# Attention and a squared-ReLU feed-forward: the first head pair in two token halves, GpSimd's loads behind it, and two units' value products moved back

## Chip, cores and metric

The kernel runs on one core of a Trainium2 chip. The metric is device time in microseconds (us) of one execution; lower is better. A profile records a single execution and gives its own span, which is a little shorter than the timed runs.

## What is computed

```python
# q, k, v: (8, 12, 448, 64) = batch, heads, tokens, head dimension; float32
scores = (1 / sqrt(64)) * q @ k.T
m = max(scores, axis=-1)
e = exp(scores - m)
attn = e / (sum(e) + exp(-m) + 1e-09)      # softmax with one more, empty, place
x = (attn @ v) as (3584, 768)              # tokens by heads * head dimension
h = x @ w_in                               # w_in: (768, 2048)
g = relu(h) ** 2
out = g @ w_out                            # w_out: (2048, 768), out float32
```

The kernel leaves out the maximum: with it both parts of the fraction scale alike, so it takes exp of the scores and adds 1 to their sum.

## The kernel before

The work is one instruction order, written out by hand: each engine (PE for matrix products, DVE and ACT for element work, POOL, SP) runs its own instructions in the order of the program, and waits on semaphores for the data of others. The attention is cut into units. A unit is one pair of heads and a range of query tokens; its scores come in two calls, `scores(u, et, 0)` and `scores(u, et, 1)`, for two chunks of 112 keys each. After them ACT takes the exp, DVE adds the chunks for the row sums, and `values` multiplies with v. The 448 tokens of a head lie as 112 partitions by 4 (`RUN = 4`, `P = 112`), four consecutive tokens in a partition.

Batch 0 is done in units 0 to 11: six pairs with the first 192 queries, then the same pairs with the other 256. Units 12 to 17 are batch 1, and from unit 18 on two units go together. In units 0 to 5 there is no product with `w_in` yet to fill PE, and `keep_warm(n)` issues n matmuls on zeros, whose results nobody reads. `drain`, from unit 7 on, issues parts of the products with `w_in` between the steps of a unit.

Loads. Pairs 0 to 2 of batch 0 come raw in float32, q from SP and k from ACT, one load for each pair and tensor (L92). They are cast on chip (`cast`, L142), transposed on PE against an identity (`transposes`, L151), and copied by DVE from PSUM to `qk`. All other q, k, v and weights of the first batches are loaded by GpSimd (POOL), which casts to float16 in the transfer (L81, L97, L103, L107). Their order in the program is: v of pairs 0 to 2 (`vn`), the identity, q and k of pair 3, of pairs 4 and 5, v of pairs 3 to 5, four eighths of `win`, q and k of batch 1's pairs 0 to 2, four more eighths, q and k of batch 1's pairs 3 to 5, v of batch 1. The tenth of these is POOL's issue L103 at 10.31 us, q and k of batch 1's pairs 3 to 5 are the seventeenth and eighteenth.

In the loop of units 0 to 11 (L451) a step is: scores of the first two chunks, the transposes of a later pair (`transpose_at`: unit i transposes pair i+1 of batch 0 up to unit 4; units 9 to 14 transpose pairs 0 to 5 of batch 1), scores of the other two chunks, then `values` of the unit before. Two units, an odd and an even before it, share one PSUM tile `xp`, which `normalise` empties before the next pair may write it. In the next loop (L495) unit 12 calls `scores(u, et, 0)`, then `transposes(1, 3)`, then half of the products left, then `scores(u, et, 1)`.

Of the kernel before, what the change touches and what calls it, by code (L numbers as in the profile page):

```python
# [8 lines left out]
FP32 = mybir.dt.float32  # L9
FP16 = mybir.dt.float16  # L10
AF = mybir.ActivationFunctionType
# [4 lines left out]
def kernel(  # L16
# [9 lines left out]
    nc = tc.nc  # L26

    B, H, S, D = q.shape
    NT, DM = out.shape
    DF = moe_w_in.shape[1]  # L30
    NPAIR = H // 2
    DCH = DM // 128
    NFFB = DF // 128
    RUN = 4
    P = S // RUN
# [8 lines left out]
    consts = ctx.enter_context(tc.tile_pool(name="consts", bufs=1))  # L44
# [4 lines left out]
    flat = ctx.enter_context(tc.tile_pool(name="flat", bufs=2))  # L49
# [22 lines left out]
    win_r = moe_w_in.rearrange("(c p) f -> p c f", p=128)  # L72
    wout_r = moe_w_out.rearrange("(c p) f -> p c f", p=128)

    whole, vns, qks, xts, naturals, stages = {}, {}, {}, {}, {}, {}

    def load_v(b, p0, p1):
        hs = slice(2 * p0, 2 * p1)
        if b not in vns:
            vns[b] = v_pool.tile([P, H, RUN, D], FP16, name="vn")  # L80
        nc.gpsimd.dma_start(out=vns[b][:, hs], in_=v_r[b, :, hs])  # L81

    def load_natural(b, p0, p1):

        raw = b == 0 and p1 <= 3
        for n, r in (("q", q_r), ("k", k_r)):
            src = r[b, :, 2 * p0:2 * p1]
            if raw:
                if p0 == 0:
                    whole[n] = e_pool.tile([P, RUN * S], FP32, name="et")  # L90
                t = whole[n][:, p0 * 512:(p0 + 1) * 512].rearrange("p (h t d) -> p h t d", h=2, t=RUN)
                (nc.sync if n == "q" else nc.scalar).dma_start(out=t, in_=src)  # L92
            else:
                if p0 % 3 == 0:
                    whole[n] = nat.tile([P, NPAIR, RUN, D], FP16, name=f"{n}n{p0 // 3}")
                t = whole[n][:, 2 * (p0 % 3):2 * (p0 % 3 + p1 - p0)]
                nc.gpsimd.dma_start(out=t, in_=src)  # L97
            for pr in range(p0, p1):
                naturals[n, b, pr] = t[:, 2 * (pr - p0):2 * (pr - p0) + 2]
# [39 lines left out]
            )  # L139


    def cast(b, pr):  # L142
        for name in "qk":
            f = flat.tile([P, 2, RUN, D], FP16, name=f"flat{name}")
            if b == 0 and pr == 0 and name == "k":
                nc.scalar.activation(out=f, in_=naturals[name, b, pr], func=AF.Copy)
            else:
                nc.vector.tensor_copy(f, naturals[name, b, pr])
            naturals[name, b, pr] = f

    def transposes(b, pr):  # L151
        tp = mp_tile(FP16)
        for i, name in enumerate("qk"):
            for s in range(RUN):
                for h in range(2):
                    nc.tensor.transpose(tp[64 * h:64 * h + 64, i, P * s:P * s + P],
                                        naturals[name, b, pr][:, h, s, :], ident[0:P, 0:P])
        if b not in qks:
            qks[b] = qk_pool.tile([128, 3, COLS], FP16, name="qk")
        parts = (0, S // 2, S) if b == 0 and pr == 0 else (0, S)  # L160
        for x, y in zip(parts, parts[1:]):
            nc.vector.tensor_copy(qks[b][:, 0:2, pr * S + x:pr * S + y], tp[:, :, x:y])

    def exp(out_, in_):
        nc.scalar.activation(out=out_, in_=in_, func=AF.Exp, scale=scale)  # L167
# [8 lines left out]
    def scores(u, et, c):  # L176
        b, pr, q0, n = u
        qk = qks[b]
        two = [] if n == S else s_psum.tile([P, 2, 512], FP32, name="sp")
        for kk in (2 * c, 2 * c + 1):  # L180
            sp = s_psum.tile([P, 2, 512], FP32, name="sp") if n == S else two
            if b in ON_PE:
                o = 0 if n == S else kk % 2 * n
                for h in range(2):
                    r = slice(64 * h, 64 * h + 64)
                    x = pr * S
                    nc.tensor.matmul(sp[:, h, o:o + n], qk[r, 1, x + P * kk:x + P * kk + P],  # L187
                                     qk[r, 0, x + q0:x + q0 + n], start=True, stop=True)
            else:
                for h in range(2):  # L190
                    for odd in range(2):
                        r = slice(64 * odd, 64 * odd + 64)
                        x = (2 * pr + h) * (S // 2)
                        kx = x + kk // 2
                        which = 1
                        if kk % 2 != odd:
                            which = 2
                            kx += kk % 2
                        nc.tensor.matmul(sp[:, odd, h * (S // 2):(h + 1) * (S // 2)],  # L199
                                         qk[r, which, kx:kx + 2 * P - 1:2], qk[r, 0, x:x + S // 2],  # L200
                                         start=True, stop=True)
            if n == S:
                exp(chunk(et, u, c, kk).rearrange("p (o x) -> p o x", o=2), sp[:, :, 0:S])
        if n < S:
            exp(et[:, 0:RUN * 2 * n].rearrange("p (c h x) -> p c h x", c=2, h=2)[:, c], two[:, :, 0:2 * n])
# [24 lines left out]
    def values(u, et, xp, o=0):  # L230
        b, pr, _, n = u
        for kk in range(RUN):
            for h in range(2):
                nc.tensor.matmul(xp[64 * h:64 * h + 64, o:o + n], vns[b][:, 2 * pr + h, kk, :],  # L234
                                 of_head(chunk(et, u, kk // 2, kk), u, h), start=(kk == 0), stop=(kk == RUN - 1))
# [119 lines left out]
    for pr in range(3):  # L355
        load_natural(0, pr, pr + 1)
    nc.scalar.preload_act_table_set("natural_log_exp_and_others")
    load_v(0, 0, 3)
    ident = consts.tile([128, 128], FP16)
    make_identity(nc, ident)  # L360
    load_natural(0, 3, 4)
    load_natural(0, 4, 6)
    load_v(0, 3, 6)
# [28 lines left out]
    def left():  # L392
        return sum(t[0] for t in ins)
# [19 lines left out]
    units = [(0, pr, 0, FIRST) for pr in range(NPAIR)] + [(0, pr, FIRST, S - FIRST) for pr in range(NPAIR)]  # L413
# [8 lines left out]
    def keep_warm(n):  # L422
        wp = m_psum.tile([128, 512], FP32, name="mp")
        for _ in range(n):
            nc.tensor.matmul(wp, warm[:, 0:128], warm, start=True, stop=True)

    share = [0.0]
    ets, ess, rcps = {}, {}, {}
    xp = None
# [12 lines left out]
        return units[i], ets[i], es, half  # L442

    keep_warm(9)
    cast(0, 0)
    transposes(0, 0)
    keep_warm(3)
    cast(0, 1)


    for i in range(2 * NPAIR):  # L451
        u, et, es, half = begin(i)
        two = units[i - 2:i] if i and i % 2 == 0 else None
        if i % 2:
            xp = x_psum.tile([128, 512], FP32, name="xp")
        mode[0] = COLS2
        scores(u, et, 0)
        if i == 0:
            keep_warm(4)
        if i == NPAIR:  # L460
            values(units[i - 1], ets.pop(i - 1), xp, units[i - 1][3])
            rcp = row_sums(two, (ess.pop(i - 2)[0:1], ess.pop(i - 1)[0:1]))
            normalise(two, xp, rcp)
            queue(0, FIRST)
            share[0] = left() / (NPAIR + 2)
        if i in transpose_at:
            transposes(*transpose_at[i])
        if i == 0:
            cast(0, 2)
        if i > NPAIR:  # L470
            drain(share[0] * 0.45)
        scores(u, et, 1)
        if 0 < i < NPAIR:
            keep_warm(1)
        if i and i != NPAIR:
            if two and i < NPAIR:
                rcp = row_sums(two, (ess.pop(i - 2)[0:1], ess.pop(i - 1)[0:1]))
            values(units[i - 1], ets.pop(i - 1), xp, (i - 1) % 2 * units[i - 1][3])
            if two and i > NPAIR:
                rcp = row_sums(two, (ess.pop(i - 2)[0:1], ess.pop(i - 1)[0:1]))  # L480
        if i > NPAIR:
            drain(share[0] * 0.3)
        add_chunks(u, et, es, half, 1)
        if two and i != NPAIR:
            normalise(two, xp, rcp)
        add_chunks(u, et, es, half, 2)
        if i > NPAIR:
            drain(share[0] * 0.25)
        if i == NPAIR + 5:
            load_natural(2, 0, 3)  # L490
            for j in range(2):
                load_wout(0, j, 2)


    for i in range(2 * NPAIR, 3 * NPAIR):  # L495
        u, et, es, half = begin(i)
        prev = units[i - 1]
        first = i == 2 * NPAIR
        if not first:
            xp = x_psum.tile([128, 512], FP32, name="xp")  # L500
# [44 lines left out]
    for c in range((NU - 3 * NPAIR) // 2):  # L545
        i = 3 * NPAIR + 2 * c
        b, pr = units[i][0:2]
# [16 lines left out]
        for at in pending:  # L564
            if at not in rcps:
                rcps[at] = row_sums([units[at]], (ess.pop(at)[0:1],))
            xp = mp_tile()
# [19 lines left out]
        n, early = ((3, 0 if b > 2 else 1), (7, 3), (6, 3))[pr // 2]  # L587
# [7 lines left out]
    for at in pending:  # L595
        xp = mp_tile()
# [36 lines left out]
```

The softmax here doesn't subtract the row's maximum and nothing guards it: scores larger than these inputs give would overflow.

## Time and profile before

| | us |
|---|---|
| median of 3 runs | 417.84 (417.56 to 418.05) |
| span of the profiled execution | 415.9 |
| PE busy | 405.5 (98%) |
| DVE busy | 278.8 (67%) |
| ACT busy | 238.4 (57%) |
| POOL busy | 36.4 (9%) |
| first 38.42 us: PE / ACT busy | 33.90 / 29.06 |
| remaining 377.48 us: PE / ACT busy | 371.64 / 209.35 |

Busy shares are means over stages that have different limits, and a PE that issues `keep_warm` counts as busy. What matters here is the front, the first 40 us: who waits for whom there, and which wait ends last. The mean granted TensorE clock is 1.000. The three DMA queues that matter are GpSimd's (software, 22.16 MB over the run), SP's (hardware, 22.05 MB, nearly all later) and ACT's (hardware, 0.69 MB, the raw k alone).

### The profile page before, as it was taken

The numbers are of one execution on the slowest core, as the hardware profiler recorded it, in microseconds if no ns is written. First come the engines' busy times: TensorE is split into PE (matmuls) and PEld (weight loads), VectorE is DVE, ScalarE is ACT, GpSimd is POOL, SyncE is SP. The second block draws the span as 40 slices with busy tenths as digits, with TensorE's granted clock in tenths as the row PEclk, the third lists the DMA queues.
The fourth block names the chain that finished last, engine by engine and source line by source line (L and its number), as shares of the span: only waits on it lengthen the run. The fifth ranks groups of instructions, "written<-read, shape, count | busy, mean of one in ns | idle before, by whom it ended". The sixth has DMA issues, their size and how long they took to land.

```text
span 415.9 us, 10695 instructions
## 1 busy us (share of the span) xinstructions
PE 405.5 (98%) x4721; PEld 256.7 (62%) x4721; DVE 278.8 (67%) x535; ACT 238.4 (57%) x329; POOL 36.4 (9%) x58
## 2 busy tenths in 40 slices
PE   8889999899999999999999999999999999999997
PEld 3567666566566666665666666665666666555664
DVE  4769888768865868568766769658676669287000
ACT  4897998664675664673576564674666655100111
POOL 7523220020000200002000400001000000000000
PEclk9999999999999999999999999999999999999999
DMA  9999999889109790199509871198101101010222
GB/s 201 197 197 198 200 197 223 159 120 199 40 2 182 139 192 6 44 199 191 123 2 164 167 151 37 39 186 154 46 2 39 39 2 39 39 39 0 77 76 77
DMA packets 75823, 45.58 MB, mean 110 GB/s; under 512 B 42560, under 2 KB 72000, under 8 KB 75456
## 3 DMA queue, kind: packets, MB, share of 16 engines
q0 software_dynamic: 28848, 22.16, 35.0%
q1 hardware_dynamic: 46208, 22.05, 23.3%
q8 instruction: 37, 0.61, 0.6%
q10 hardware_dynamic: 720, 0.69, 0.6%
q14 instruction: 10, 0.08, 0.1%
HBM read 45.69 MB, written 17.93 MB: 153 GB/s over the span
## 4 chain that ended last, share of the span: by engine, by line
PE 86%; DMA 9%; ACT 2%; DVE 2%; issue 1%; POOL 0%; POOLq 0%
PE mp L284 23%; PE mp L330 17%; PE mp L286 11%; PE xp L284 8%; PE sp L199 6%; PE xp L330 6%; PE mp L234 5%; DMA kn<-in_k_dram 4%; PE xp L286 3%; DMA win<-in_moe_w_in_dram 3%; PE xp L234 3%; PE sp L187 2%; DMA vn<-in_v_dram 2%; PE mp L248 2%; ACT et L167 1%
## 5 line engine op out<-in xcount | busy, mean ns | idle before, releaser
L167 ACT ACTIVATE et<-sp 112x896 f16<-112x896 f32 (+2 forms) x192 | 165.8, 914 | 55.6 <-PE sp L199 40.1
L284 PEld LDWEIGHTS <-win 128*64 128x64 f16 x1536 | 85.3, 110 | 45.7 <-issue 2.8
L284 PE MATMUL mp<-xt,win 128*64 128x448 f16 (+2 forms) x1236 | 110.2, 324 | 1.5 <-DVE xt L263 0.8
L330 PE MATMUL mp<-wout,gs 64*128 64x384 f16 x864 | 102.3, 322 | 0.0
L330 PEld LDWEIGHTS <-gs 64*128 64x128 f16 x1152 | 56.1, 94 | 31.7
L301 DVE TENSOR_SCALAR rt<-mp 128x448 f16<-128x448 f32 (+2 forms) x99 | 61.6, 622 | 17.4 <-PE mp L284 13.3
L303 DVE TENSOR_TENSOR gs<-rt 128x448 f16<-128x448 f16 (+2 forms) x128 | 50.2, 392 | 4.4
L330 PE MATMUL xp<-wout,gs 64*128 64x384 f16 x288 | 52.6, 322 | 0.0
L251 ACT ACTIVATE rcp<-mp,one_b 128x448 f32<-128x448 f32 (+2 forms) x40 | 25.1, 629 | 40.1 <-PE mp L248 35.8
L212 DVE TENSOR_TENSOR es<-et 112x896 f16<-112x896 f16 x42 | 26.0, 620 | 17.7 <-ACT et L167 17.6
L339 ACT ACTIVATE ot<-mp 128x384 f32<-128x384 f32 (+1 forms) x29 | 14.1, 487 | 36.2 <-PE mp L286 27.6
L199 PE MATMUL sp<-qk 64*112 64x224 f16 x480 | 33.8, 260 | 0.0
L286 PEld LDWEIGHTS <-gs 128*128 128x128 f16 x256 | 24.4, 98 | 15.1 <-issue 0.4
L284 PE MATMUL xp<-xt,win 128*64 128x448 f16 x300 | 32.6, 352 | 0.0
L199 PEld LDWEIGHTS <-qk 64*112 64x112 f16 x480 | 26.3, 128 | 9.7 <-issue 5.4
L234 PEld LDWEIGHTS <-vn 112*64 112x64 f16 x432 | 22.1, 109 | 15.3 <-issue 5.2
L286 PE MATMUL mp<-wout,gs 128*128 128x384 f16 (+1 forms) x192 | 31.0, 322 | 0.0
L341 DVE SCALAR_TENSOR_TENSOR ot<-mp,ot 128x384 f32<-128x384 f32 x27 | 15.1, 558 | 21.7 <-PE sp L199 11.6
L252 ACT ACTIVATE rcp<-rcp 128x448 f32<-128x448 f32 (+2 forms) x48 | 27.7, 577 | 1.5
L214 DVE TENSOR_TENSOR es<-es,half 112x896 f16<-112x896 f16 x42 | 26.2, 625 | 1.4
L212 DVE TENSOR_TENSOR half<-et 112x896 f16<-112x896 f16 x42 | 25.9, 616 | 0.3 <-ACT et L167 0.3
L301 DVE TENSOR_SCALAR rt<-xp 128x448 f16<-128x448 f32 x29 | 18.0, 622 | 12.0 <-PE xp L286 8.3
(61 smaller groups left out, 313.9 us busy)
## 6 DMA issues: line engine op xcount, KB each, us to landing
vn<-in_v_dram POOLq DMA_DIRECT2D x7, 672.0 KB, 9.0
out_dram<-ot SPq DMA_DIRECT2D x9, 384.0 KB, 2.8
win<-in_moe_w_in_dram POOLq DMA_DIRECT2D x8, 384.0 KB, 13.9
wout<-in_moe_w_out_dram POOLq DMA_DIRECT2D x4, 768.0 KB, 12.8
stage_q<-in_q_dram POOLq DMA_DIRECT2D x4, 676.0 KB, 10.9
stage_k<-in_k_dram POOLq DMA_DIRECT2D x4, 676.0 KB, 13.3
out_dram<-ot SPq DMA_DIRECT2D x8, 288.0 KB, 3.2
out_dram<-ot SPq DMA_DIRECT2D x9, 192.0 KB, 2.7
```

What stands on the lines that cost most here:

```text
L167: nc.scalar.activation(out=out_, in_=in_, func=AF.Exp, scale=scale)
L199: nc.tensor.matmul(sp[:, odd, h * (S // 2):(h + 1) * (S // 2)], qk[r, which, kx:kx + 2 * P - 1:2], qk[r, 0, x:x + S // 2], start=True, sto ...
L212: nc.vector.tensor_add((es, half[:, 0:2 * S])[step], e[:, 2 * step], e[:, 2 * step + 1])
L214: nc.vector.tensor_add(es, es, half[:, 0:2 * S])
L234: nc.tensor.matmul(xp[64 * h:64 * h + 64, o:o + n], vns[b][:, 2 * pr + h, kk, :], of_head(chunk(et, u, kk // 2, kk), u, h), start=(kk == 0 ...
L251: nc.scalar.activation(out=rcp[:, 0:m], in_=zp[:, 0:m], func=AF.Ln, bias=one_b)
L252: nc.scalar.activation(out=rcp[:, 0:m], in_=rcp[:, 0:m], func=AF.Exp, scale=-1.0)
L284: nc.tensor.matmul(out_[x:x + 64], lhsT[:, x:x + 64], rhs, start=start, stop=stop)
L286: nc.tensor.matmul(out_, lhsT, rhs, start=start, stop=stop)
L301: nc.vector.tensor_scalar(out=rt[:, 0:m], in0=hp[:, 0:m], scalar1=0.0, scalar2=None, op0=ALU.max)
L303: nc.vector.tensor_mul(gs[:, f0:f0 + per, t0 % RING:t0 % RING + n], r, r)
L330: nc.tensor.matmul(o[:, 0:w], g[x:x + 64], wout[x:x + 64, fb, n0:n0 + w], start=(fb == 0), stop=(fb == NFFB - 1))
```

## The change

Pair 0 of batch 0 is loaded, cast, transposed and copied in two halves of two tokens per partition (tokens 0 to 223 and 224 to 447 of the transposed order). A one-element copy on POOL, reading k of pair 0 in its second half, stands ahead of all of GpSimd's loads; the identity is made ahead of that copy. Unit 0's second scores stand directly behind its first, with fewer `keep_warm` matmuls about them (3 and 4 become 1, 1 and 2). Pair 1's copy to `qk` is in two halves. `values` of units 2 and 4 no longer stand at the end of units 3 and 5, but behind the first scores of units 4 and 6.

```diff
+    HALVES = ((0, RUN // 2), (RUN // 2, RUN))
...
-                (nc.sync if n == "q" else nc.scalar).dma_start(out=t, in_=src)
+                for s0, s1 in HALVES if p0 == 0 else ((0, RUN),):
+                    (nc.sync if n == "q" else nc.scalar).dma_start(out=t[:, :, s0:s1], in_=src[:, :, s0:s1])
...
-    def cast(b, pr):
+    fp16s = {}
+
+    def cast(b, pr, s0=0, s1=RUN):
         for name in "qk":
-            f = flat.tile([P, 2, RUN, D], FP16, name=f"flat{name}")
-            if b == 0 and pr == 0 and name == "k":
-                nc.scalar.activation(out=f, in_=naturals[name, b, pr], func=AF.Copy)
+            if s0 == 0:
+                fp16s[name, b, pr] = flat.tile([P, 2, RUN, D], FP16, name=f"flat{name}")
+            f, t = fp16s[name, b, pr][:, :, s0:s1], naturals[name, b, pr][:, :, s0:s1]
+            if pr == 0 and name == "k":
+                nc.scalar.activation(out=f, in_=t, func=AF.Copy)
             else:
-                nc.vector.tensor_copy(f, naturals[name, b, pr])
-            naturals[name, b, pr] = f
-
-    def transposes(b, pr):
+                nc.vector.tensor_copy(f, t)
+
+    def transposes(b, pr, s0=0, s1=RUN):
...
-        parts = (0, S // 2, S) if b == 0 and pr == 0 else (0, S)
-        for x, y in zip(parts, parts[1:]):
-            nc.vector.tensor_copy(qks[b][:, 0:2, pr * S + x:pr * S + y], tp[:, :, x:y])
+        for x, y in HALVES if b == 0 and pr == 1 else ((s0, s1),):
+            nc.vector.tensor_copy(qks[b][:, 0:2, pr * S + P * x:pr * S + P * y], tp[:, :, P * x:P * y])
...
-    load_v(0, 0, 3)
     ident = consts.tile([128, 128], FP16)
     make_identity(nc, ident)
+    seen = consts.tile([1, 1], FP32)
+    nc.gpsimd.tensor_copy(seen, whole["k"][0:1, RUN * D - 1:RUN * D])
+    load_v(0, 0, 3)
...
-    cast(0, 0)
-    transposes(0, 0)
-    keep_warm(3)
+    for part in HALVES:
+        cast(0, 0, *part)
+    for part in HALVES:
+        transposes(0, 0, *part)
+    keep_warm(1)
     cast(0, 1)
...
         if i == 0:
-            keep_warm(4)
+            keep_warm(1)
+            scores(u, et, 1)
+            keep_warm(2)
+        if two and i in (4, NPAIR):
+            values(two[0], ets.pop(i - 2), xp)
...
-        scores(u, et, 1)
+        if i:
+            scores(u, et, 1)
...
-            values(units[i - 1], ets.pop(i - 1), xp, (i - 1) % 2 * units[i - 1][3])
+            if i not in (3, 5):
+                values(units[i - 1], ets.pop(i - 1), xp, (i - 1) % 2 * units[i - 1][3])
```

More of the change, by code (lines that the diff above doesn't have):

```diff
@@ L139, in transposed_loads @@
             )
-    def cast(b, pr):
+    fp16s = {}
+    def cast(b, pr, s0=0, s1=RUN):
         for name in "qk":
-            f = flat.tile([P, 2, RUN, D], FP16, name=f"flat{name}")
-            if b == 0 and pr == 0 and name == "k":
-                nc.scalar.activation(out=f, in_=naturals[name, b, pr], func=AF.Copy)
-            else:
-                nc.vector.tensor_copy(f, naturals[name, b, pr])
-            naturals[name, b, pr] = f
-    def transposes(b, pr):
+            if s0 == 0:
[3 more added lines that the diff above has]
+                nc.scalar.activation(out=f, in_=t, func=AF.Copy)
+            else:
+                nc.vector.tensor_copy(f, t)
+    def transposes(b, pr, s0=0, s1=RUN):
         tp = mp_tile(FP16)
[L153 to L157, printed above, removed]
         if b not in qks:
             qks[b] = qk_pool.tile([128, 3, COLS], FP16, name="qk")
-        parts = (0, S // 2, S) if b == 0 and pr == 0 else (0, S)
-        for x, y in zip(parts, parts[1:]):
-            nc.vector.tensor_copy(qks[b][:, 0:2, pr * S + x:pr * S + y], tp[:, :, x:y])
+        for i, name in enumerate("qk"):
+            for s in range(s0, s1):
+                for h in range(2):
+                    t = fp16s.get((name, b, pr), naturals[name, b, pr])
+                    nc.tensor.transpose(tp[64 * h:64 * h + 64, i, P * s:P * s + P], t[:, h, s, :], ident[0:P, 0:P])
+        for x, y in HALVES if b == 0 and pr == 1 else ((s0, s1),):
+            nc.vector.tensor_copy(qks[b][:, 0:2, pr * S + P * x:pr * S + P * y], tp[:, :, P * x:P * y])
     def exp(out_, in_):
```

## The prediction

> **What bounds the kernel now.** I read the chain of work that ended last first, because TensorE is busy 98% of the span by part 1 of the page and that says nothing of the first microseconds. The chain is 86% PE, but it does not begin there:
>
> ```profile
> PE 86%; DMA 9%; ACT 2%; DVE 2%; issue 1%; POOL 0%; POOLq 0%
> ```
>
> The same chain in order of time, cut to its first 42 us (start, length, what):
>
> ```profile
> 1.30 7.92 DMA vn<-in_v_dram
> ...
> 10.31 12.93 DMA win<-in_moe_w_in_dram
> ...
> 23.82 14.56 DMA kn<-in_k_dram
> 38.38 0.04 issue
> 38.42 0.39 PE mp L156 x8
> 38.81 1.32 PE mp L284 x32
> ```
>
> So up to 38.4 us the end is set by one thing: the queue of GpSimd's loads, from its first issue (values of pairs 0 to 2) to the landing of K of batch 1, pairs 3 to 5. After that the chain is PE, ACT and DVE with no DMA in it. The place where the two meet is in PE's timeline (start, length, idle before and releaser in brackets):
>
> ```profile
> 37.75 0.39 PE L156 MATMUL mp<-ident,qn 112*64 112x112 f16 x8
> 38.42 0.39 PE L156 MATMUL mp<-ident,kn 112*64 112x112 f16 x8 [0.28 <-DMA kn<-in_k_dram]
> 38.64 1.49 PE L284 MATMUL mp<-xt,win 128*64 128x192 f16 x32
> ```
>
> PE comes to transposes(1, 3), in unit 12, at 37.75, and waits 0.28 us for K. Instructions run in order, so nothing passes this point before that load has landed, however early PE comes. Everything after it is the same program before and after the change.
>
> Third, how fast that queue moves. Over the first 8 us, by queue (packets, MB, share), and then in windows (PE, PEld, DVE, ACT and POOL busy, clock, DMA share, GB/s):
>
> ```profile
> q0 software_dynamic: 479, 0.25, 22.6%
> ```
>
> ```profile
> 8.00:9.00 1.00, 0.78 (x20) 0.50 (x18) 0.48 (x1) 0.18 (x1) 0.03 (x1) 1.00 1.45 196
> 9.00:10.00 1.00, 0.80 (x18) 0.55 (x20) 1.00 (x4) 1.00 (x2) 0.49 (x1) 1.00 1.45 193
> 10.00:12.00 2.00, 2.00 (x41) 1.29 (x38) 1.73 (x4) 1.56 (x3) 2.00 (x4) 1.00 1.45 196
> ```
>
> From 8 us on it moves a steady 193 to 203 GB/s until 40 us, with no gap: bandwidth sets the landings, not issue. Taken back from 8 us (0.25 MB at 0.198 MB/us are 1.26 us), the stream behaves as if it had run at full rate since **6.74 us**. A later effective start moves every landing behind it by as much.
>
> Fourth, who goes first. The six SP and ACT loads of the raw pairs 0 to 2 are issued from 0.74 on. The trace has no GpSimd packet before 5.46 us, although vn is issued at 1.30 and takes 0.89 us to issue. Those loads are therefore not slowed by GpSimd's in the first 5 us; only the last one, K of pair 2, shares with it (its packets run from 6.0 to 8.0). The converse is there too: an output store issued at 90.80, amid GpSimd packets, has its first packet 3.70 us later, against about 0.85 us for stores on idle engines. What reaches the engines first is served first.
>
> **What the Trainium skill says.** "DMA: Bandwidth & Descriptors", Issuing engines are not separate DMA queues: loads of SP, ACT and GpSimd run on the same 16 DMA engines and interleave. The trace agrees that they share, but shows the late one queueing for microseconds. The same page, Specifications, gives about 1 us to a GpSimd load's first byte; this trace shows 1.67 us from issue to first packet in all five later loads of vn, which I use. It also gives 512 B as the least size at line rate; the halves are just 512 B runs, and the trace has 27 ns for a 512 B packet and 46 ns for one of 1,024 B on the SP queue, so halving costs 8 ns a pair. "TensorE: Matmul & The Clock Gate", The HAM clock gate: the clock falls back after an idle window of about 3.4 us. The clock is 1.00 in every window here, and the longest PE wait in the first 40 us is 0.8 us after its start, so no run yet shows the limit.
>
> **The change part by part.**
>
> *The gate on GpSimd.* POOL now makes the identity first and then copies one element of the second half of K of pair 0. Behind that copy on POOL stand vn, q and k of pair 3, pairs 4 and 5, and all of win: the whole queue above. When is it free? In before, ACT's cast of the same K starts at 4.86 when it lands. Two halves add 28 x 27 - 14 x 46 ns = 0.11 us for each of q and k on each engine, 0.22 us in all: 5.08. The copy costs 0.18 to 0.38 us (the five L435 rows), and in those rows a load follows 0.57 us or more after the copy's start, some of it another wait; I take 0.4. So vn is issued at about 5.5 (bounds 5.0 and 5.8) in place of 1.30.
>
> From issue to full rate: a queue that starts on idle engines ramps. vn of a later batch, issued at 140.48:
>
> ```profile
> 142.00:142.50 0.50, 0.50 (x8) 0.31 (x6) 0.50 (x2) 0.00 (x0) 0.44 (x1) 1.00 0.52 47
> 142.50:143.00 0.50, 0.50 (x10) 0.31 (x6) 0.47 (x3) 0.00 (x0) 0.00 (x0) 1.00 0.66 44
> 143.00:143.50 0.50, 0.50 (x10) 0.27 (x7) 0.50 (x2) 0.00 (x0) 0.00 (x0) 1.00 0.81 76
> 143.50:144.00 0.50, 0.50 (x8) 0.38 (x6) 0.47 (x3) 0.31 (x1) 0.00 (x0) 1.00 1.18 131
> 144.00:144.50 0.50, 0.50 (x10) 0.29 (x6) 0.50 (x1) 0.47 (x2) 0.00 (x0) 1.00 1.36 185
> 144.50:145.00 0.50, 0.50 (x10) 0.27 (x7) 0.41 (x2) 0.50 (x2) 0.00 (x0) 1.00 1.47 201
> ```
>
> The six sum to 0.342 MB by 145.0, which is 1.73 us at full rate: effective start 143.27, or 2.8 us after issue, of which 1.67 us is to the first packet and 1.1 us the ramp. In before the ramp lay behind SP's and ACT's packets. After the change those drain at about 6.7: 5.5 us plus 328 packets that are left then at some 360 a microsecond, plus 0.2 us for the halves. vn's first packet would come at 5.5 + 1.67 = 7.2, when they are gone. With the whole ramp exposed the effective start is 8.3, 1.55 us later than 6.74; with all of it hidden, 7.2, 0.45 us later. As some reads can be queued while the tail drains, I take **1.1 us**; bounds -0.1 (issue at 5.0, nothing exposed) and 1.6. A gain beyond 0.1 is excluded: SP's and ACT's bytes have to move in either case, and full rate from 6.7 on is no more than before had.
>
> *The halves, casts and transposes.* ACT and SP issue one load more each, 0.48 us, which puts off their loads of pairs 1 and 2 and, on ACT, the table load (2.24, 1.28 us), to end near 4.0; the first halves land at about that time and pair 1 is wanted at 6.2, so this lies beside the wait. Before, the cast of q starts at 4.49, that of k ends at 5.49, the copies run 5.97 to 6.66, and the first exp starts at 7.03. After: PE is held by the nine warm matmuls to 5.05 anyway; first-half transposes to 5.45, copy 0.35 to 5.8, scores 5.85, exp near 6.3, 0.7 us earlier. The second scores now stand ahead of transposes(0, 1), with two warm matmuls for four, so the second exp follows at 7.1 in place of 8.82. DVE then binds: copies 0.7, casts of pair 1 0.9, copies 0.7, casts of pair 2 0.85, additions 0.9 us from 5.5 put its next copy at 10.0 in place of 10.59. The front gains **0.6 to 1.3 us**; bounds 0 and 2, since ACT idles 2.4 us between 7.03 and 30. Splitting pair 1's copy adds about 0.07 us on DVE (0.69 for 0.62).
>
> *Values of units 2 and 4 moved.* 8 matmuls, 0.52 us, move from units 3 and 5 to 4 and 6; nothing is added. It removes PE's wait of 0.79 us for the normalisation at 19.48, but ACT idles only 0.17 us before its next exp at 20.40, so ACT hides most: 0 to 0.5 us earlier. No DMA moves with it.
>
> *Sum at unit 12.* PE arrives 0.6 to 1.5 us early, K lands 1.1 us late. The end moves with K: 0 + 1.1 = +1.1 us; the early arrival becomes a longer wait, 0.28 + 1.1 + about 1 = 2.4 us, still under the skill's window. Part of the front's gain goes sooner: K of pairs 4 and 5 lands at 13.0 now and would land at 14.1, where unit 3 needs it at 13.8. The profiled span, 415.9, becomes 417.0; the unprofiled median, 417.84, moves by the same 1.1, to **418.9**.
>
> **Rivals.** *A, the stream loses little* (-0.1 to +0.8 us): the ramp is a matter of idle engines and the tail of SP's and ACT's packets hides it. For: in before the stream starts amid them without a dip. Against: the tail ends before vn's first packet. Likeliest 0.4: 418.2. *B, faster*: the wait at unit 12 is no bound, K lands at least 0.84 us early, and the front's gain passes on; 417.84 - 1.1 = 416.7. It decides once the effective start is before 5.9 us, so vn would have to be issued by 4.2 at the latest with no ramp at all. Against: K of pair 0 is not there before 4.86 now, and GpSimd's packets took nothing from it. *C, a cold start*: if the 4.16 us from first issue to first packet were GpSimd's own start and not the queue ahead of it, the gate would cost 5.5 + 4.16 - 5.46 = 4.2 us less the hidden ramp: 421 to 422. The store of 90.80 speaks against it. *D*: the dependence is not tracked by region, and POOL waits for all raw K, whose packets end at 8.0 in before: vn issued at 7.5 or later, +2 us or more. The first cast starts at 4.49, before the later pairs land, which speaks against it.
>
> **How the numbers follow.** About 0.2% (0.84 us) is what a measurement here can tell from no change. Main case, +0.8 to +1.6 us: 0.55. A: 0.27, nearly all within 0.84. B: 0.10. C and D: 0.08. Faster 0.10, same 0.27, slower 0.63. Main and A hold 0.82: low 417.6, high 419.8, which leaves out B, C and D.
>
> **What would show it.** Right: the first GpSimd packet near 7.2; DMA under 150 GB/s around 7 us; the landing in front of transposes(1, 3) at 39 to 40, with a PE wait there of 1.5 to 2.5 us; the first exp before 6.6. The remainder after that point should stay 377.5 us. Wrong: K of batch 1 landing by 38.4 or earlier, or PE passing unit 12 without a DMA wait.

## The result, and the profile after

The changed kernel took 420.01 us in the median of four executions (419.05 to 420.86), the kernel before 417.85 (417.56 to 418.05): a ratio of 1.0052, 95% interval 1.0028 to 1.0076. It is slower by 2.2 us where 1.1 were forecast. Eight more executions on another chip gave 418.87 (418.55 to 420.85) against 417.83, ratio 1.0032 [1.0020, 1.0044]. All twelve together have a median of 419.1. They spread over 2.3 us, the 21 executions of before that ran beside the eight over 0.9; part of the question is what spreads them.

The chain of work that ended last, by engine, in the first profile after:

```profile
PE 89%; ACT 4%; DVE 3%; DMA 2%; issue 1%; ACTq 0%; DVEq 0%
```

DMA has fallen from 9% to 2%: here the chain no longer runs through GpSimd's loads, but through PE, ACT and DVE of the front. PE at unit 12, from its timeline:

```profile
39.50 0.39 PE L164 MATMUL mp<-ident,qn 112*64 112x112 f16 x8
39.86 0.39 PE L164 MATMUL mp<-ident,kn 112*64 112x112 f16 x8
40.08 1.49 PE L288 MATMUL mp<-xt,win 128*64 128x192 f16 x32
```

PE is at this point 1.75 us later than in before (37.75), not earlier, and K is 1.39 us later (last packet 39.44 for 38.05), so that they nearly meet. In the profile of the repeat (after_again, below) PE comes at 38.86 and waits:

```profile
38.86 0.39 PE L164 MATMUL mp<-ident,qn 112*64 112x112 f16 x8
39.72 0.39 PE L164 MATMUL mp<-ident,kn 112*64 112x112 f16 x8 [0.47 <-DMA kn<-in_k_dram]
```

From the start of K's transposes to the end of the span it is 417.2 - 39.86 = 377.3 us after and 415.9 - 38.42 = 377.5 before; over all profiles taken it stays between 377.2 and 377.5. The whole difference therefore lies ahead of that instruction. The timeline of after shows the gate, and two places where the front lost time:

```profile
4.52 0.18 POOL L365 COPY seen<-et 1x1 f32<-1x1 f32 x1 [3.21 <-DMA et<-in_k_dram]
4.64 0.91 POOL L82 DMA_DIRECT2D vn<-in_v_dram  x1
...
7.50 0.43 DVE L154 CAST flatq<-et 112x512 f16<-112x512 f32 x1 [1.03 <-DMA et<-in_q_dram]
...
15.05 0.39 PE L164 MATMUL mp<-ident,kn 112*64 112x112 f16 x8 [0.32 <-DMA kn<-in_k_dram]
```

vn is issued 3.34 us later (4.64 for 1.30). DVE waits 1.03 us for q of **pair 1**, which SP loads itself: the cast starts at 7.50. In before it started at 6.58 and waited for no data:

```profile
6.58 0.72 DVE L148 CAST flatq<-et 112x512 f16<-112x512 f32 x1
```

And unit 3 waits for K of pairs 4 and 5, which before had been there. The windows of the same kernel (columns as before; the clock is the third number from the end) show one thing more:

```profile
20.00:22.00 2.00, 1.29 (x22) 0.97 (x22) 1.39 (x4) 2.00 (x3) 0.82 (x1) 1.00 1.45 197
22.00:24.00 2.00, 1.67 (x18) 1.23 (x18) 0.47 (x2) 1.53 (x4) 0.65 (x1) 0.68 1.46 197
24.00:26.00 2.00, 1.84 (x18) 0.97 (x16) 1.48 (x3) 2.00 (x3) 0.82 (x2) 0.50 1.45 199
26.00:28.00 2.00, 2.00 (x38) 1.50 (x36) 1.31 (x3) 1.23 (x2) 1.02 (x2) 0.96 1.45 197
```

The TensorE clock fell to half for 3.4 us, from 22.7 to 26.1 (mean over the span 0.996). No execution of before shows less than 0.999.

### The profile page after: what moved, and what is told of

It is laid out like the page before. It is cut to its first block, busy times and chain, and to the rows that moved or that the text cites. A ratio compares the mean times of both kernels' runs of the same rounds, so it can differ in the third digit from the quotient of the medians.

```text
span 417.2 us, 10697 instructions
## 1 busy us (share of the span) xinstructions
PE 406.7 (97%) x4718; PEld 257.2 (62%) x4718; DVE 279.0 (67%) x537; ACT 238.6 (57%) x330; POOL 36.5 (9%) x59
## 4 chain that ended last, share of the span: by engine, by line
PE 89%; ACT 4%; DVE 3%; DMA 2%; issue 1%; ACTq 0%; DVEq 0%
PE mp L288 24%; PE mp L334 17%; PE mp L290 11%; PE xp L288 8%; PE sp L203 6%; PE xp L334 6%; PE mp L238 5%; PE xp L238 3%; PE xp L290 3%; PE sp L191 3%; ACT et L171 2%; PE mp L252 2%; DMA et<-in_k_dram 2%; PE mp L164 1%; DVE qk L166 1%
## 5 line engine op out<-in xcount | busy, mean ns | idle before, releaser
L191 PE MATMUL sp<-qk 64*112 64x448 f16 (+2 forms) x192 | 24.5, 328 | 3.1 <-ACT et L171 2.2
L216 DVE TENSOR_TENSOR half<-et 112x896 f16<-112x896 f16 x42 | 25.9, 616 | 0.3 <-ACT et L171 0.3
## 6 DMA issues: line engine op xcount, KB each, us to landing
win<-in_moe_w_in_dram POOLq DMA_DIRECT2D x8, 384.0 KB, 13.7
stage_k<-in_k_dram POOLq DMA_DIRECT2D x4, 676.0 KB, 13.7
```

The costliest lines, as they stand in the source:

```text
L216: nc.vector.tensor_add((es, half[:, 0:2 * S])[step], e[:, 2 * step], e[:, 2 * step + 1])
```

## The experiments

There were three theories at first. **1**: the gate delays GpSimd's stream, and K of batch 1 sets the end. **2**: the clock falls. **3**: the split of pair 0's loads delays SP's and ACT's own loads behind them (3a), or the new order of casts, scores and warm matmuls does the harm (3b). **4** and **5**, on how a split could do that, were formed later. A "full clock" below is a mean of 0.999 or 1.000 over the execution. Each kernel was timed beside the kernel before on its chip, which stood at 417.75 to 417.83.

**The change once more** (after_again). No edit.

> The changed kernel once more, beside its three single parts, to see how far its time spreads and which of its executions have a clock under 1. Theory 1 (the gate moves GpSimd's stream and nothing else moves the end): K of batch 1, pairs 3 to 5, has its last packet 1.0 to 2.2 us later than the 38.05 us of before, and the spans follow it, 1 to 2.5 us above before, also in executions with clock 1.000. Theory 2 (the TensorE clock falls to half for 3.4 us): spans with clock 1.000 stand within 0.5 us of before, those under 1 stand above.

Measured: 418.87, K's last packet at 39.39 (+1.34 us), end of the span 417.1. Of eight executions seven have a clock of 0.999 or 1.000 and take 418.55 to 419.16; the eighth has 0.987 and takes 420.85. With a full clock K is late as theory 1 says, and the clock comes on top. The first four had clocks of 0.996, 1.000, 1.000 and 0.992; its two of 1.000 took 420.35 and 419.67, which the clock does not explain.

**Single parts.** The gate alone, on the kernel before (gate_only):

```diff
-    load_v(0, 0, 3)
     ident = consts.tile([128, 128], FP16)
     make_identity(nc, ident)
+    seen = consts.tile([1, 1], FP32)
+    nc.gpsimd.tensor_copy(seen, whole["k"][0:1, RUN * D - 1:RUN * D])
+    load_v(0, 0, 3)
```

> The kernel before with the gate alone (pair 0 whole, so the copy waits for all of K of pair 0). Theory 1: the first GpSimd packet at about 7 us in place of 5.46, K lands 1.0 to 2.0 us later, time 418.8 to 420. Theory 3 (halves): K within 0.5 us of before, time under 418.4.

Measured: 419.17 (418.73 to 420.87, 6 runs), 1.0038 [1.0026, 1.0050]. The first GpSimd packet comes at 6.83, K's last at 39.74, and PE waits for it:

```profile
38.88 0.39 PE L156 MATMUL mp<-ident,qn 112*64 112x112 f16 x8
40.10 0.39 PE L156 MATMUL mp<-ident,kn 112*64 112x112 f16 x8 [0.83 <-DMA kn<-in_k_dram]
```

The gate alone is worth +1.3 us, and K is late by the mechanism of the prediction (+1.7 us). That PE, too, comes late in this profile (38.88 for 37.75) has in part to do with how the execution began. At the start a warm matmul takes some 0.43 us (nine in 3.92), later half of that. In before the pace had changed by the three warm matmuls behind the first transposes, here it had not. Before, then gate_only:

```profile
5.87 0.82 PE L425 MATMUL mp<-warm 128*128 128x512 f16 x3
...
6.21 1.31 PE L427 MATMUL mp<-warm 128*128 128x512 f16 x3
```

The first exp started 0.83 us later (7.86 for 7.03). So a late PE in one profile need not be the work of the edit.

The changed kernel without the gate (no_gate):

```diff
+    load_v(0, 0, 3)
     ident = consts.tile([128, 128], FP16)
     make_identity(nc, ident)
-    seen = consts.tile([1, 1], FP32)
-    nc.gpsimd.tensor_copy(seen, whole["k"][0:1, RUN * D - 1:RUN * D])
-    load_v(0, 0, 3)
```

> The changed kernel without the copy on POOL, vn issued first again. Theory 1 (the gate): K lands at 38.0 to 38.4, time within 0.5 us of before, 417.4 to 418.4. Theory 3 (the halves delay SP's and ACT's own loads of pairs 1 and 2, and all behind them, with or without the gate): K lands at 38.8 or later, time 418.6 or more. Theory 2 (clock): clock under 1 in some executions and 418.5 or more in those.

Measured: 421.08 (418.99 to 422.63, 6 runs), 1.0074 [1.0048, 1.0099]: slower than with the gate. Five of six executions have a clock of 0.988 to 0.996. The one with a full clock took 419.12. In its profile vn is issued first again, and K is as late as with the gate (last packet 39.67):

```profile
40.01 0.39 PE L164 MATMUL mp<-ident,kn 112*64 112x112 f16 x8 [0.57 <-DMA kn<-in_k_dram]
```

So the halves delay K without the gate, as theory 3 expected, and the two delays do not add up. The gate is not the only cost; with the halves in place the kernel with it is even the faster one, as its clock falls more seldom (three of twelve executions).

Values of units 2 and 4 alone (values_only):

```diff
+        if two and i in (4, NPAIR):
+            values(two[0], ets.pop(i - 2), xp)
...
-            values(units[i - 1], ets.pop(i - 1), xp, (i - 1) % 2 * units[i - 1][3])
+            if i not in (3, 5):
+                values(units[i - 1], ets.pop(i - 1), xp, (i - 1) % 2 * units[i - 1][3])
```

> The kernel before with values of units 2 and 4 moved, nothing else. Theory 1: K lands as before and sets the end, so 417.6 to 418.1. Theory 2 (the moved products leave TensorE idle long enough in units 3 to 6 for the clock to fall): clock under 1.000 in some executions, and 418.5 or more in those.

Measured: 417.74 (13 runs), 1.0001 [0.9993, 1.0009], clock 0.999 or 1.000 throughout. No effect.

**The loads against the computing.** Only pair 0's loads split, all else as before (load_halves):

```diff
-                (nc.sync if n == "q" else nc.scalar).dma_start(out=t, in_=src)
+                for s0, s1 in ((0, 2), (2, 4)) if p0 == 0 else ((0, RUN),):
+                    (nc.sync if n == "q" else nc.scalar).dma_start(out=t[:, :, s0:s1], in_=src[:, :, s0:s1])
```

> The kernel before with nothing changed but the four loads of pair 0 (two token halves of q and k each); casts, transposes and copies take whole tiles. Theory 3a (the split loads are the cost, in whatever order the rest stands): q and k of pair 1 land 0.8 us or more later than in before, K of batch 1 lands at 38.7 or later, time 418.5 to 421. Theory 3b (the cost comes from the new order of casts, scores and warm matmuls): all landings within 0.3 us of before, time within 0.4 us of it.

Measured: **422.88** (418.91 to 424.07, 6 runs), 1.0100 [1.0066, 1.0133]. Four loads of pair 0 in place of two, two of them in each queue, cost 5 us by themselves, the clock that falls with them included (five of six executions; the sixth took 418.91). The DVE timeline shows where the front waits:

```profile
8.00 0.43 DVE L149 CAST flatk<-et 112x512 f16<-112x512 f32 x1 [0.71 <-DMA et<-in_k_dram]
...
10.59 0.43 DVE L149 CAST flatq<-et 112x512 f16<-112x512 f32 x1 [1.05 <-DMA et<-in_q_dram]
```

and the windows what follows the waits:

```profile
8.00:10.00 2.00, 1.24 (x24) 0.62 (x18) 1.05 (x2) 0.79 (x1) 0.00 (x0) 1.00 1.33 232
10.00:12.00 2.00, 0.65 (x16) 0.48 (x16) 1.42 (x3) 0.82 (x2) 1.36 (x2) 1.00 1.45 195
12.00:14.00 2.00, 2.00 (x23) 1.03 (x17) 1.62 (x5) 0.81 (x1) 1.82 (x3) 0.56 1.45 197
...
24.00:26.00 2.00, 2.00 (x19) 1.19 (x17) 0.82 (x2) 1.96 (x4) 0.82 (x2) 0.53 1.45 197
26.00:28.00 2.00, 1.84 (x30) 1.20 (x28) 0.92 (x2) 1.61 (x3) 0.88 (x1) 1.00 1.45 197
```

q of pair 2 has its last packet at 10.1 where before it was 6.4. PE is busy 1.9 of the 4 us from 8 to 12, and then runs at half clock for 13.7 us. In that profile K has its last packet at 38.58 and PE comes to unit 12 at 43.65: the end is the front's.

Split by head instead, with runs of 1,024 bytes (load_heads):

```diff
-                (nc.sync if n == "q" else nc.scalar).dma_start(out=t, in_=src)
+                for h0, h1 in ((0, 1), (1, 2)) if p0 == 0 else ((0, 2),):
+                    (nc.sync if n == "q" else nc.scalar).dma_start(out=t[:, h0:h1], in_=src[:, h0:h1])
```

> As load_halves, but pair 0 split by head, so that its runs stay 1,024 bytes and each load has half the packets. If the number of loads in a queue is the cause (the third load of a queue starts late and cold): as load_halves, 418.5 to 421. If the 512-byte packets are: as before, 417.5 to 418.3.

Measured: 420.68 (417.89 to 423.20, 15 runs), 1.0065 [1.0043, 1.0088]; so a split into runs of 1,024 bytes costs as well, not only small packets. Six executions with a full clock took 417.89 to 419.85, nine with 0.983 to 0.992 took 420.29 to 423.2.

The computing in halves, pair 0 loaded whole, no gate (compute_halves, the changed kernel without the gate and with this taken back):

```diff
-                for s0, s1 in HALVES if p0 == 0 else ((0, RUN),):
-                    (nc.sync if n == "q" else nc.scalar).dma_start(out=t[:, :, s0:s1], in_=src[:, :, s0:s1])
+                (nc.sync if n == "q" else nc.scalar).dma_start(out=t, in_=src)
```

> The changed kernel without its gate and with pair 0 loaded whole: only casts, transposes and scores in halves, fewer warm matmuls, values moved. Theory 1 (K of batch 1 sets the end): the front runs early, by 0.3 to 1.5 us at unit 11, K lands at 38.0 to 38.3 and PE waits for it by as much; time within 0.4 us of before. Theory 2 (clock): under 1.000 in some executions, and those 1 us or more above.

Measured: 417.70 (13 runs), 1.0000 [0.9992, 1.0008], no fallen clock. Half of the expectation failed: the front is not early. PE comes to transposes(1, 3) at 38.30, not before 37.75, and does not wait there. The second exp is early (7.70 for 8.82), but the next unit's starts at 9.53 for 9.61, since it waits for pair 1 and for DVE. Later PE waits twice for ACT, 0.94 and 0.90 us, behind the moved values of units 2 and 4 (values_only has the same two waits). Theory 3b is out.

**How the split does it.** In before two loads per queue carry pairs 0 and 1, and GpSimd's first packet comes at 5.46, when they are nearly through. With the split it comes at 3.7 (load_halves, load_heads and no_gate alike), when pair 0 is nearly through and pair 1's q has begun. That suggests that each queue has two loads at the engines and the rest joins later, side by side with GpSimd's (theory 4). Theory 5 is that the number of loads in a queue costs by itself. Three loads, pair 0 in halves and pairs 1 and 2 in one:

```diff
-    for pr in range(3):
-        load_natural(0, pr, pr + 1)
+    load_natural(0, 0, 1)
+    load_natural(0, 1, 3)
```

(the tile's slice then runs to `p1 * 512`), on top of load_halves (load_halves_merged):

> load_halves with pairs 1 and 2 in one load for each tensor, so that SP and ACT have three loads each again, as in before; pair 0 stays in 512-byte halves. Theory 4 (a queue keeps two loads under way; the rest waits for them and then starts cold, so that the third load of four is the late one): with three the large third load still starts behind the halves, and its pair 1 is no earlier than in load_halves: 419 to 423. Theory 5 (the number of loads by itself): back to 417.5 to 418.5.

Measured: 425.27 (422.48 to 426.22, 6 runs), 1.0161 [1.0137, 1.0185]. The third load has its last packet at 10.2 (q) and 11.0 (k). There are three loads per queue again, as in before, and it is slower still: theory 5 is out. The same edit with pair 0 whole, two loads per queue (load_merged):

> The kernel before with pairs 1 and 2 in one load for each tensor, two loads in SP's and ACT's queues. Theory 4: no load is third, both start at once and without a gap between them; K of batch 1 lands within 0.3 us of before or up to 0.5 us sooner, but pair 1 is seen only when pair 2 has landed as well, near 7 to 8 us, 0.5 to 1 us later than it is wanted: 417.5 to 419. Theory 5: as before or better.

Measured: 418.16 (417.77 to 422.27, 22 runs), 1.0026 [1.0010, 1.0042]. GpSimd's first packet comes at 6.15, later than in before, with ACT's last quarter still to come (its last packet is at 7.46); K's last is at 37.91. 17 executions with a full clock took 417.77 to 418.46, five with a fallen one up to 422.27: the clock can fall without a split. The times are as theory 4 expects, but it is a reading of when packets start, not of the queues themselves, and two things do not fit a third load that stands back. SP's third load begins right behind its second in before (4.91) and in load_halves (3.32), ahead of GpSimd's first packet. And GpSimd need not be there: in the changed kernel it moves nothing before 6.76, and pair 1 is late all the same. What is low there is the rate of SP's and ACT's loads: 256 GB/s from 3 to 4 us, where before has 369, and in the next microsecond (before, then after):

```profile
4.00:5.00 1.00, 1.00 (x3) 0.15 (x1) 0.51 (x1) 0.14 (x1) 1.00 (x3) 1.00 1.10 311
...
4.00:5.00 1.00, 1.00 (x3) 0.15 (x1) 0.29 (x1) 0.86 (x3) 0.48 (x2) 1.00 0.66 184
```

In the repeat it is 246 and 286 GB/s. Theory 4 is not shown.

**How much is the clock.** load_halves with six warm matmuls ahead of the transposes of units 0 and 1 (load_halves_warm):

```diff
+        if i in (0, 1):
+            keep_warm(6)
         if i in transpose_at:
             transposes(*transpose_at[i])
```

> load_halves with six more warm matmuls ahead of the transposes of units 0 and 1, where PE waits for pair 2. Theory 2 (most of the cost of the late loads is the clock that falls in that wait): no execution under 0.998, time 418 to 420. If the late data is the cost itself: 421 to 424 as in load_halves, whatever the clock.

Measured: 420.15 (419.89 to 420.24, 5 runs), 1.0054 [1.0042, 1.0066], clock 0.999 or 1.000. Of the 5.1 us of load_halves 2.7 are gone with the clock held; 2.4 stay for the late data and the extra matmuls, which this run does not tell apart. The spread went from 5 us to 0.35.

The changed kernel with more warm matmuls in units 1 to 5 (after_warm):

```diff
         if 0 < i < NPAIR:
-            keep_warm(1)
+            keep_warm(3)
```

> The changed kernel with three warm matmuls in place of one in units 1 to 5. Theory 2 (the executions of 419.7 to 420.9 are those whose clock fell): no execution under 0.998 and none above 419.6, median 418.6 to 419.4, as the two more cost at most 0.4 us a unit where PE has time. If the slow executions have another cause, some at 420 and above remain with a full clock.

Measured: 419.19 (419.00 to 419.26, 5 runs), 1.0033 [1.0021, 1.0045]. No clock falls, and no execution is above 419.3.

**K out of the way.** The changed kernel with K of batch 1 loaded earlier (after_k_early):

```diff
-    for i in range(4, 8):
+    for i in range(4, 6):
         load_win(i, 8)
     load_natural(1, 3, 6)
+    for i in range(6, 8):
+        load_win(i, 8)
```

> The changed kernel with q and k of batch 1's pairs 3 to 5 ahead of the last two eighths of win. If K's landing sets the end of the changed kernel (theory 1), the wait of some 0.8 us in unit 12 goes and the time falls to 418.0 to 418.4 in executions with a full clock; if the late front alone sets it, it stays at 418.6 to 419.4.

Measured: 418.12 (417.16 to 421.81, 22 runs), 1.0023 [1.0007, 1.0039]. With a full clock (15 executions) the median is 417.86, against 418.84 for the seven of the changed kernel (on another chip): 1.0 us, as theory 1 says. The clock fell in seven, median 420.86.

The same edit on the kernel before (k_early), on compute_halves (compute_k_early) and on load_merged (merged_k_early):

> The kernel before with q and k of batch 1's pairs 3 to 5 ahead of the last two eighths of win. The wait of 0.28 us in unit 12 goes, so 417.3 to 417.7; if the landing of the last eighths is waited for, above 418.

Measured: **417.30** (417.04 to 422.26, 14 runs), 0.9990 [0.9982, 0.9999]. Thirteen executions with a full clock took 417.04 to 418.07, median 417.15; after_k_early, on the same chip, stands 0.7 us above that. This is what the change costs beside K's landing. In the fourteenth the clock fell to a mean of 0.984, and this is the one that was profiled: there DVE waited for k of pair 2, cast at 10.37 where before it was 9.39, and from 11.5 us on the clock was at half. Neither split nor gate is in this kernel, so late loads and a fallen clock can come without them, though no execution of before on record has a fallen clock.

> compute_halves with q and k of batch 1's pairs 3 to 5 loaded ahead of the last two eighths of win. Theory 1: K lands near 34.6, the wait in unit 12 goes, and the front's gain passes on to the end: 416.4 to 417.5. If the front is bound by something else by then, 417.5 to 418.2; if the last eighths of win are then waited for, above 418.

Measured: 417.55 (13 runs), 0.9995 [0.9987, 1.0003]; the halves in the computing and the moved values gain nothing here; all had a full clock, and they stand 0.4 us above those of k_early.

> load_merged with q and k of batch 1's pairs 3 to 5 ahead of the last two eighths of win, so that K is out of the way. Time is then the front's own: 417.0 to 417.8 if load_merged makes the front no later, 418 to 419 if pair 1 is seen late.

Measured: 418.01 (417.75 to 422.64, 13 runs), 1.0020 [1.0001, 1.0040]; the clock fell in two. It is hardly better than load_merged, which fits a front that sets the end, as expected where pair 1 is seen late.

## Why the prediction was right and wrong

**The chain and its meeting point: right.** The whole difference lies ahead of transposes(1, 3), and the remainder stayed within 0.3 us. Taking K out of the way gave back 1.0 us.

**The gate: right in kind, its share not separable.** +1.1 us was forecast for K; +1.34 and +1.39 were measured in the changed kernel, +1.69 with the gate alone, +1.62 with the halves and no gate, and +0.53 in load_halves (one profile of each). So with a full clock the total, +1.0 us in the seven executions, came out near the forecast in part by luck: without the gate K was as late. As a shift of GpSimd's stream the forecast was good: by 12 us it had moved 1.02 MB in before, 0.80 with the gate alone and 0.84 in the changed kernel, which at some 0.196 MB/us is 1.1 and 0.9 us late. Two terms of the working were off against each other. vn was issued at 4.64, not 5.5, for the copy started at 4.52 and the load followed 0.12 us later, without the 0.4 that was allowed. First packet 6.76 for 7.2. But the rate then came up slowly: in the repeat, all queues together, 157 GB/s from 7 to 8 us and 188 in the next, where before has 235 and 196. The ramp was wholly exposed: 0.84 MB by 12 us put the effective start at 7.7, 3.1 us after the issue, where the working had 2.8 with the whole ramp.

**The halves: the step that failed.** The prediction said that the additional load on each queue "lies beside the wait", since pair 1 is wanted at 6.2, and that the front gains 0.6 to 1.3 us. Pair 0 did gain: the exps of unit 0 began at 6.64 and 7.34 for 7.03 and 8.82, and K's second half was there at 4.46, ahead of the whole K in before (4.84). But pair 1 lost more. Its q had its last packet at 5.98 for 5.16, and the last of its sixteen completion signals at 7.47 for 5.90 (7.66 in the repeat); fifteen had come by 6.67, and why one was so late is not known. DVE cast it at 7.50 for 6.58, unit 1's exp began at 9.88, not before 9.61, and PE came to unit 12 at 39.50 (with the 3.4 us at half clock) and 38.86, that is 1.75 and 1.1 us late, where 0.6 to 1.5 early was forecast. In place of "0 + 1.1" at that point there stand two late arrivals, of which the later counts. The price of a split was put at 0.22 us for small packets; load_halves measured +5.1 us and load_heads +2.9, and both come with late loads behind pair 0. The sign was in the prediction's own reading: in before K of pair 2, third in its queue, shared the engines with GpSimd (as did q of pair 2, from 5.46 to 6.4, which the reading missed). With the split, pair 1 stands third.

**The clock: the term that was missing.** It was put at nothing. The working compared the longest single wait with the Trainium skill's idle window of 3.4 us ("TensorE: Matmul & The Clock Gate", The HAM clock gate). The traces differ from it: in load_halves no wait of PE from 5 to 13 us is longer than 1.1 us, and the clock fell after 4 us in which PE was busy 1.9. In the changed kernel it fell in three of twelve executions (0.996, 0.992, 0.987), worth some 2 us in the repeat (420.85 against 418.84). Removing three warm matmuls was not by itself the cause: compute_halves removes them too and keeps its clock. That the late data bring the fall is what the order of events in load_halves suggests, and added matmuls stop it (load_halves_warm, after_warm).

**The values: harmless here, as forecast,** though not early: the wait of 0.79 us went, and PE waited 0.94 and 0.90 us for ACT in two later steps instead. At unit 12 it was 0.5 us late (38.27 for 37.75), and the wait for K took that up.

**Rivals.** A, that the tail of SP's and ACT's packets hides the ramp, does not fit gate_only (+1.3 us, K +1.7). B fails at its own point: vn would have had to be issued by 4.2. C did not happen: the first packet came 2.1 us after vn's issue, not 4.16. Nor did D: the copy ran at 4.52. None of them was the split.

**Open.** Two executions of the first four took 419.67 and 420.35 with a full clock, and no trace of them exists. The median of 420.01 lies between these two, so how much of it is late data, and why more than in the repeat, is not shown; load_heads, too, spreads over 2 us with a full clock. Why a split makes the loads behind it slow is open, and so is why the halves delay K without the gate. Why the clock falls in some executions and not in others of one kernel was not settled. In the traces it changes in steps of 3.41 us, counted from a start that differs by execution and lies between 3.9 and 7.2 us of the span. In the four that fell before 13 us PE was busy 0.9 to 2.4 us of the step just before. But 2.39 fell (load_merged) and 2.35 did not (no_gate), so PE's busy time alone does not decide it.

## What to carry to other kernels

Before a load is split, ask what then stands behind it in its queue, and who is waiting for that; the bytes were the same here, and the split alone cost 1%, more than half of which went when added matmuls held the clock. A gate on a queue whose landings are set by bandwidth, as here, pays its delay again at the far end of that queue, so look there for a consumer that already waits. When two edits are made together, run each without the other: here K was as late without the gate, and with the gate alone, as with all of it. Where TensorE fills its waits with little, read the mean clock of every execution along with the time: a median over both kinds hides two effects.

## What the runs showed of the hardware

- A fallen clock stayed down while PE was busy without a gap: in load_halves it was at 0.50 from 12.2 to 25.9 us, though PE shows 2.00 of 2.00 in every window between. In before the clock was at 1.00 over the same stretch.
- The mean clock took few values, 0.996, 0.992, 0.988 and 0.984 and near them (down to 0.976 in load_halves_merged), as one to four (there six) steps of 3.4 us at half clock in some 417 would give (1.7 of 417 is 0.4%). In load_heads the median of those near 0.992 was 420.7, of those near 0.984 it was 422.6.
- The mean clock leaves out the slow start. In gate_only, with a mean of 0.999, three warm matmuls at 6.21 us took 1.31 us where in before, at 5.87, they took 0.82; the first exp came 0.83 us later.
- One load's sixteen completion signals need not come together. For pair 1's q in the changed kernel fifteen had come by 6.67 us and the last at 7.47; in before all came between 4.95 and 5.90.
